# A layer norm's root moved to VectorE, a feature map in one tile, and an earlier modulation sum, in an attention and GLU kernel

## The chip, the cores and the metric

The kernel runs on one core of one Trainium2 chip. The metric is the device time of one execution in microseconds. A core has TensorE (PE: matmuls and transposes, with its weight loads as PEld), VectorE (DVE), ScalarE (ACT), GpSimd (POOL) and SyncE (SP), which here issues DMAs. Each engine works through its own instructions in order and waits at an instruction until the data and buffers it needs are ready.

## The reference

One block with conditioning: a modulation vector gives a shift, a scale and a gate for each of two halves. The first half is an attention over 4 segments of 512 tokens with 32 heads of width 16 and a running memory; the second a bilinear GLU. Sizes: x is 2048 × 512, the GLU's width 1376.

```python
mod = silu(c) @ w_mod                       # 6 vectors of 512: sa, ca, ga, sb, cb, gb
h = layernorm(x) * (1 + ca) + sa
# per segment s, q, k, v = h @ wq, h @ wk, h @ wv, 32 heads of 16
p = softmax(q @ k.T * scale + mask)         # inside the segment; masked where query < key
phi = lambda t: where(t > 0, t + 1, exp(t)) # feature map of the memory
a_mem = (phi(q) @ M) / (phi(q) @ z + 1e-6)  # memory of the earlier segments
o = g * a_mem + (1 - g) * (p @ v);  M += phi(k).T @ v;  z += sum(phi(k))
x = x + ga * (o @ wo)
h = layernorm(x) * (1 + cb) + sb
x = x + gb * (((h @ w_gate) * (h @ w_up)) @ w_down)
```

## The kernel before

The attention stage lasts from about 50 to 520 us and the GLU stage from there to the end; before 50 us weights are loaded and the first segment is projected. Attention is a loop over 32 half groups of 4 heads, each in 5 slots (0 to 4). A slot has a first score matmul `q` (queries against keys, which gives VectorE the row maxima `nm`), later a second one, `k`, with the maxima included, whose exponential on ScalarE is the tile `pt` (L329), which GpSimd masks with selects (L332); `tb` multiplies `pt` with the values.

Between these, a generator `fill_a` hands out work for the rest of the block: the projections `a_kq` of keys and queries of a segment (`kps`, `qps`, copied to `f`), the feature map phi, the memory `a_mem` (matmuls `mp`, `up`, `mz`), the layer norm of the next segment's rows (`ln_rows`, tiles `ast`, `amv`, `ay` and `x`; `cst`, `cmv`, `cy` for the norm in front of the GLU) and the modulation vectors. `weave(gen, other, places)` lets one step of `other` run at each listed yield of `gen`; a number listed twice takes two steps there. The order on TensorE is written out by these generators. The other engines are ordered by a scheduler, with some instructions pinned to where the program issues them (`pin`), or behind the last `pt` exponential (`behind`).

`ln_rows` takes the statistics of four row blocks (`BATCH_NORM_STATS2` and an aggregate, one step each), then Ln and Exp on ScalarE give 1/sqrt(var) as `y`, and one Newton step refines this root in five operations on 128 × 4 elements; only then is each block `x` normalized on VectorE. In the first norm of all, the five are on VectorE (`CV`), in the seven others on GpSimd (L187 to L191).

`mod_acc` makes one modulation vector from four blocks of `w_mod`: ScalarE scales block k by `s_c` (L626, in place, tile `wm`) and GpSimd adds it to block 0 (L628); the matmuls `mc` then turn the sum into columns. In segments 1 and 2 a second such vector is made inside the projections of group 1.

phi is built as min(exp(f), 1) + max(f, 0): ScalarE writes relu to `rl` (one buffer, L814) and the exponential to `ph` (L815), VectorE joins them later. The tile `f` has two buffers.

Of the kernel before, what the change touches and what calls it, by code (L numbers as in the profile page):

```python
# [9 lines left out]
F32 = mybir.dt.float32  # L10
F32R = mybir.dt.float32r
BF = mybir.dt.bfloat16
AF = mybir.ActivationFunctionType
ALU = mybir.AluOpType
# [4 lines left out]
P = 128  # L19
# [39 lines left out]
def tile_kernel(ctx, tc, x, wq, wk_, wv, wo, beta, w_gate, w_up, w_down, c, w_mod, out):  # L59
# [107 lines left out]
    def ln_rows(pool, xt, s, pfx):  # L167

        first = pfx == "a" and s == 0
        V, A = (CV, CA) if first else (vec, act)  # L170
        mv = pool.tile([P, 4, 2], F32, tag="mv", name=f"{pfx}mv{s}", bufs=2)
        for t in range(4):
            st = pool.tile([P, 6], F32, tag="st", name=f"{pfx}st{s}_{t}", bufs=2)
            i = V.bn_stats(st, xt[t])
            if not first:
                pin(i)
            V.bn_aggr(mv[:, t, :], st)
            if not first:
                yield 0.0
        sd = pool.tile([P, 4], F32, tag="sd", name=f"{pfx}sd{s}", bufs=2)  # L180
        A.activation(sd, mv[:, :, 1], AF.Ln, bias=epst[:, 0:1])
        y = pool.tile([P, 4], F32, tag="y", name=f"{pfx}y{s}", bufs=2)
        A.activation(y, sd, AF.Exp, scale=-0.5)
        a = pool.tile([P, 4], F32, tag="ya", name=f"{pfx}ya{s}", bufs=2)
        b = pool.tile([P, 4], F32, tag="yb", name=f"{pfx}yb{s}", bufs=2)
        eng = CV if first else nc.gpsimd
        eng.tensor_mul(a, y, y)  # L187
        eng.tensor_scalar(b, mv[:, :, 1], 1.0, EPS, op0=ALU.mult, op1=ALU.add)
        eng.tensor_mul(b, b, a)
        eng.tensor_scalar(b, b, -0.5, 1.5, op0=ALU.mult, op1=ALU.add)  # L190
        eng.tensor_mul(y, y, b)  # L191
        yield 0.0
        for t in range(4):
            i = V.tensor_scalar(xt[t], xt[t], mv[:, t, 0:1], y[:, t:t + 1],
                                op0=ALU.subtract, op1=ALU.mult)
            if not first:
                pin(i)
                yield 0.0
        if first:
            yield 0.0  # L200
# [382 lines left out]

    xts = {0: xload(0)}
    NWU = 20
    wu = pa.tile([P, 512], BF, tag="rl", name="wu", bufs=1)
    vec.memset(wu, 0.0)
    wups = psp.tile([P, 2, 512], F32, tag="lk", name="wups", bufs=1)

# [97 lines left out]
                i += 1  # L687

    wH, wL = {}, {}
    stage = [("ph", 3), ("ph", 3), ("ph", 3), ("mem", 2), ("pkr", 1), ("f", 2)] + [("x", 4)] * 6  # L690
    nst = [0]

    def staged(nm):
# [65 lines left out]
    def a_kq(s, g, nm):  # L759

        hH, hL = hcur[0]
        ph = phs.setdefault((s, g), {})
        if True:
            dst = kd if nm == "k" else qd
            ps = bank(f"{nm}ps{s}_{g}")
            n = 0
            for k in range(KT):
                for a, b in ((wH, hH), (wL, hH), (wH, hL)):
                    MM(ps, a[nm, g][:, k, :], b[k], start=n == 0, stop=n == 11)
                    n += 1  # L770
                    if n in (3, 6, 9):
                        yield 0.68
            give()
            f = pa.tile([P, L], F32, tag="f", name=f"{nm}f{s}_{g}", bufs=2)
            fast = s == 0 and g == 0
            A, V = (CA, CV) if fast else (act, nc.gpsimd)
            A.activation(f, ps, AF.Copy)
            q3 = pa.tile([P, 3, L], BF, tag="q3", name=f"{nm}3_{s}_{g}", bufs=2)
            r = pa.tile([P, L], F32, tag="qr", name=f"{nm}r_{s}_{g}", bufs=2)

            def part0():
                behind(A.activation(q3[:, 0, :], f, AF.Copy))
                V.tensor_sub(r, f, q3[:, 0, :])

            if fast:
                part0()
            else:
                keep(part0)

            def rest():  # L790
                (CV.tensor_copy if fast else act.copy)(q3[:, 1, :], r)
                V.tensor_sub(q3[:, 2, :], r, q3[:, 1, :])
                for r0, n, k in ((0, 3, 0), (3, 2, 0), (5, 1, 0)) if nm == "k" else ((0, 1, 3), (3, 1, 2), (5, 1, 1)):
                    if nm == "k":
                        nc.sync.dma_start(dst[s][g][r0:r0 + n].rearrange("r p t -> p r t"), q3[:, 0:n, :])
                    else:
                        i = 3 - k
                        nc.sync.dma_start(dst[s][g][r0:r0 + k].rearrange("r p t -> p r t"),
                                          q3[:, i:i + 1, :].to_broadcast([P, k, L]))

            if fast:
                rest()
            phi = (nm == "k" and s < NSEG - 1) or (nm == "q" and s > 0)
            if phi:
                if fast:
                    yield 0.0
                phlog.append((s, g, nm))
                while memq and (s == NSEG - 1 and g > 0 or len(phlog) > 3 and phlog[-4] not in phdone):
                    yield mem_step() or 0.0
                e = pa.tile([P, L], F32, tag="ph", name=f"ph{nm}{s}_{g}", bufs=3)  # L810
                rl = pa.tile([P, L], F32, tag="rl", name=f"rl{nm}{s}_{g}", bufs=1)

                def phi0():
                    behind(act.activation(rl, f, AF.Relu))  # L814
                    behind(act.activation(e, f, AF.Exp))  # L815

                if fast:
                    phi0()
                else:
                    keep(phi0)  # L820
                ph[nm] = e
            yield 0.68
            if not fast:
                give()
                rest()
            if phi:
                later.append([lambda: pin(vec.scalar_tensor_tensor(e, e, 1.0, rl, op0=ALU.min, op1=ALU.add)), 0, nm])
                if fast:
                    flush("kq")
        nkq[s, g] = nkq.get((s, g), 0) + 1  # L830
        if nkq[s, g] == 2:
            done.add((s, g))
# [127 lines left out]
    def fill_a():  # L960
# [5 lines left out]
        for s in range(NSEG):  # L966
# [4 lines left out]
            for g in range(2 if s == 0 else 0, NG):  # L971
                ws = []
                if s == 0 and g < 3:
                    ws = [load_g(nm, w, g + 1) for nm, w in (("k", wk_), ("q", wq))]
                for w in ws:
                    next(w)
                K, Q = a_kq(s, g, "k"), a_kq(s, g, "q")
                if g >= 2 and s + 1 < NSEG:
                    if g == 2:
                        xts[s + 1] = xload(s + 1)  # L980
                        lns = a_ln(s + 1)
                        K = weave(K, lns, (2, 3) if s > 0 else (3,))
                        Q = weave(Q, lns, (0, 1, 2) if s > 0 else (0, 1, 2, 3))
                    else:
                        K = weave(K, lns, (1, 1, 2, 2))
                        Q = weave(Q, lns, (0, 1, 2, 3))
                if g == 1 and 0 < s < 3:
                    acc = mod_acc(r)
                    K, Q = weave(K, acc, (0, 2)), weave(Q, acc, (0, 2))
                if s == NSEG - 1 and g == 1:  # L990
                    xr0 = xr_load(0, wpool, (0, 1), "wor")
                    ready = chain(wo_weights(), wo_op(0, None, B["orl"], us[0]))
                if s == NSEG - 1 and 0 < g < NG - 1:
                    K, Q = weave(K, ready, (0, 2)), weave(Q, ready, (0, 2) if g == 1 else (0, 2, 3))
                if s == NSEG - 1 and g == NG - 1:
                    yield from weave(Q, ready, (0, 1, 2, 3))
                    memq.append(a_mem(s, g))
                    yield from K
                    yield from ready
                    yield from wo_mm(0, us[0], xr0, (0, 1))  # L1000
                    break
                yield from K
                for w in ws:
                    next(w)
                yield from Q
                if s > 0 and g == 0:
                    while vfree[0] < s:
                        yield None
                    if s < 3:
                        yield from weave(a_v(s), mod_acc(r), (1, 3, 5, 7))  # L1010
                        yield from a_mod(2 * s, r[0])
                        r = load_mod(2 * s + 1)
                    else:
                        yield from a_v(s)
                        B["orl"] = wo_load(0, wpool)
                if g == 1 and 0 < s < 3:
                    yield from a_mod(2 * s + 1, r[0])
                memq.append(a_mem(s, g))
# [501 lines left out]
```

## Time and profile before

| What | Value |
| --- | --- |
| Median of 3 runs | 876.64 us |
| Lowest and highest | 872.87, 876.84 us |
| Profiled execution, its own time | 873.19 us |
| Its span in the trace | 871.1 us |
| Busy: PE, DVE, ACT, POOL | 828.9, 658.9, 474.5, 423.3 us |
| Mean granted clock of TensorE | 0.995 |

The span runs from the first to the last instruction in the trace; 2.1 us of the profiled execution lie outside it. Everything in the trace belongs to this one execution. A row of the timeline has the start in us, the duration, the engine, the line, the operation, what it writes and reads, and in brackets how long the engine had stood before it and what released it. In a window's row the granted clock is the share of TensorE's full clock that the throttle allowed.

### The profile page before, as it was taken

The numbers are of one execution on the slowest core, as the hardware profiler recorded it, in microseconds if no ns is written. First come the engines' busy times: TensorE is split into PE (matmuls) and PEld (weight loads), VectorE is DVE, ScalarE is ACT, GpSimd is POOL, SyncE is SP. The second block draws the span as 40 slices with busy tenths as digits, with TensorE's granted clock in tenths as the row PEclk, the third lists the DMA queues.
The fourth block names the chain that finished last, engine by engine and source line by source line (L and its number), as shares of the span: only waits on it lengthen the run. The fifth ranks groups of instructions, "written<-read, shape, count | busy, mean of one in ns | idle before, by whom it ended". The sixth has DMA issues, their size and how long they took to land.

```text
span 871.1 us, 14342 instructions
## 1 busy us (share of the span) xinstructions
PE 828.9 (95%) x4823; PEld 581.2 (67%) x4824; DVE 658.9 (76%) x1728; ACT 474.5 (54%) x740; POOL 423.3 (49%) x564
## 2 busy tenths in 40 slices
PE   8989998989999899999988899999999999999998
PEld 5756565656565566655654577888778888887886
DVE  8688776988779877789888769888685966767532
ACT  3758757687676876678544664433354423333321
POOL 4536536565455764487323835998101755650000
PEclk9999999999999999999999999999999999999999
DMA  7773755567647565776794552654305232112032
GB/s 242 227 233 120 226 149 168 187 209 232 194 147 250 188 205 168 250 235 215 235 310 134 170 173 97 181 159 135 109 30 163 77 115 55 50 55 94 0 119 97
DMA packets 111355, 139.45 MB, mean 160 GB/s; under 512 B 18800, under 2 KB 70000, under 8 KB 111280
## 3 DMA queue, kind: packets, MB, share of 16 engines
q1 hardware_dynamic: 106016, 130.91, 48.7%
q10 hardware_dynamic: 5264, 7.62, 2.4%
q8 instruction: 38, 0.62, 0.3%
q14 instruction: 37, 0.30, 0.1%
HBM read 87.48 MB, written 50.76 MB: 159 GB/s over the span
## 4 chain that ended last, share of the span: by engine, by line
PE 66%; DVE 13%; ACT 7%; DMA 5%; POOL 3%; issue 3%; SPq 0%; ACTq 0%; POOLq 0%; DVEq 0%
PE g L90 23%; PE acc L90 14%; PE tb L90 5%; PE k L90 5%; PE q L90 5%; DVE q L40 4%; PE vps L90 4%; PE kps L90 2%; ACT pt L329 2%; PE wops L90 2%; PE qps L90 2%; DVE x L40 2%; DMA x1d<-xr 1%; DMA x<-in_x_dram 1%; PE mz L90 1%
## 5 line engine op out<-in xcount | busy, mean ns | idle before, releaser
L40 DVE CUSTOM_DVE_ANT_0 q<-q,cmask 128x384 f32<-128x384 f32 (+3 forms) x512 | 246.6, 508 | 57.7 <-PE q L90 47.8
L329 ACT ACTIVATE pt<-k 128x1024 f32<-128x1024 f32 x160 | 163.9, 1024 | 74.2 <-PE k L90 57.3
L332 POOL TENSOR_SCALAR_AFFINE_SELECT pt<-pt 128x256 f32<-128x256 f32 (+1 forms) x224 | 105.2, 484 | 154.9 <-ACT pt L329 149.8
L90 PE MATMUL q<-kst,qst 96*128 96x384 bf16 (+3 forms) x512 | 101.6, 300 | 12.1 <-DVE nm L40 11.5
L90 PE MATMUL k<-qst,kst 98*128 98x384 bf16 (+3 forms) x512 | 97.5, 303 | 9.4 <-ACT pt L329 9.1
L448 POOL TENSOR_TENSOR w<-w 128x256 f32<-128x256 f32 (+1 forms) x84 | 73.9, 893 | 56.0 <-DVE t L1205 37.9
L443 POOL TENSOR_TENSOR AL<-w,AH 128x512 fp32r<-128x512 f32 (+1 forms) x42 | 56.4, 1345 | 48.4 <-ACT AH L439 48.3
L90 PE MATMUL tb<-pt,v 128*32 128x512 f32 (+3 forms) x1024 | 77.4, 443 | 1.4 <-POOL pt L332 1.4
L90 PEld LDWEIGHTS <-kst 98*128 98x128 bf16 x512 | 38.5, 99 | 54.3 <-issue 48.0
L40 DVE DVE_READ_ACCUMULATOR2_ANT nm<- 128x1 f32 x512 | 72.3, 141 | 0.0
L90 PEld LDWEIGHTS <-qst 96*128 96x128 bf16 x512 | 43.4, 98 | 39.9 <-issue 15.9
L439 ACT ACTIVATE AH<-w 128x512 fp32r<-128x512 f32 (+3 forms) x88 | 47.2, 565 | 40.0 <-POOL w L448 26.7
L1462 DVE TENSOR_TENSOR mL<-mid,mH 128x512 fp32r<-128x512 f32 (+1 forms) x44 | 32.8, 750 | 41.5 <-ACT mH L1461 41.5
L90 PE MATMUL acc<-DH,mL 128*128 128x512 f32 x144 | 56.6, 393 | 0.9 <-DVE mL L1462 0.9
L90 PE MATMUL acc<-DH,mH 128*128 128x512 f32 x144 | 57.2, 397 | 0.0
L90 PEld LDWEIGHTS tb<-pt,v 128*32 128x32 f32 x1024 | 29.2, 111 | 41.1 <-issue 36.1
L90 PE MATMUL acc<-DL,mH 128*128 128x512 f32 x144 | 56.6, 393 | 0.0
L1461 ACT ACTIVATE mH<-mid 128x512 fp32r<-128x512 f32 (+1 forms) x44 | 27.1, 627 | 52.7 <-PE acc L90 51.5
L1254 ACT ACTIVATE p<-g 128x512 f32<-128x512 f32 (+1 forms) x22 | 13.1, 597 | 75.9 <-PE g L90 75.8
L443 DVE TENSOR_TENSOR AL<-w,AH 128x512 fp32r<-128x512 f32 (+3 forms) x44 | 35.2, 803 | 9.2 <-ACT AH L439 9.0
L358 ACT ACTIVATE tsb<-tb 128x512 f32<-128x512 f32 x32 | 19.1, 598 | 34.0 <-PE tb L90 34.0
L90 PE MATMUL g<-chH,AH 128*128 128x512 f32 (+1 forms) x88 | 34.8, 396 | 0.7 <-ACT p L1254 0.7
(286 smaller groups left out, 2064.3 us busy)
## 6 DMA issues: line engine op xcount, KB each, us to landing
kst<-kd SPq DMA_DIRECT2D x32, 384.0 KB
qst<-qd SPq DMA_DIRECT2D x32, 384.0 KB
td<-tsb ACTq DMA_DIRECT2D x28, 256.0 KB
wm<-in_w_mod_dram SPq DMA_DIRECT2D x24, 256.0 KB
kd<-k SPq DMA_DIRECT2D x16, 384.0 KB
qd<-q SPq DMA_DIRECT2D x16, 384.0 KB
w<-in_w_gate_dram SPq DMA_DIRECT2D x20, 256.0 KB
w<-in_w_up_dram SPq DMA_DIRECT2D x40, 128.0 KB
```

What stands on the lines that cost most here:

```text
L40: i = getattr(self.eng, name)(*a, **k)
L90: return pe(nc.tensor.matmul(*a, **k))
L329: lpt[0] = act.activation(pt, kp, AF.Exp, scale=0.25)
L332: sels[u, i] = nc.gpsimd.affine_select(w, w, pattern=[[0, w.shape[1]], [1, P]], compare_op=ALU.is_ge, fill=0.0, base=0, channel_multiplier=-1)
L358: act.activation(tsbs[u], tbs.pop(u), AF.Copy)
L439: i = act.activation(hi[sl], w[sl], AF.Copy)
L443: i = eng.tensor_sub(lo[sl], w[sl], hi[sl].bitcast(F32))
L448: i = ce.tensor_tensor(w[:, o, :, 0:n], w[:, x, :, 0:n], w[:, y, :, 0:n], op=op)
L1254: lcp[0] = act.activation(r["p1"], ps, AF.Copy)
L1461: pin(act.activation(mH[0:n], md[0:n], AF.Copy))
L1462: vec.tensor_sub(mL[0:n], md[0:n], mH[0:n].bitcast(F32))
```

## The change

Four edits. The feature map becomes max(f, 0) + exp(−relu(−f)), which is the same function: ScalarE writes relu(−f) to `ph` and the exponential in place, the tile `rl` is gone, and VectorE reads `f` itself, which therefore is held longer and gets a third buffer. The root of the seven later norms is refined on VectorE in four operations (two of the five are joined in one), pinned ahead of the first normalization; the step's yield moves ahead of them. The norm of segment 1's rows, woven into segment 0's third group, takes its statistics steps at other yields: none in K, five in Q. And the second modulation vector of segments 1 and 2 takes three of its four steps in K (yields 1, 2, 3) and one in Q, where it had two in each. The startup tile `wu` shares another tag.

```diff
         b = pool.tile([P, 4], F32, tag="yb", name=f"{pfx}yb{s}", bufs=2)
-        eng = CV if first else nc.gpsimd
-        eng.tensor_mul(a, y, y)
-        eng.tensor_scalar(b, mv[:, :, 1], 1.0, EPS, op0=ALU.mult, op1=ALU.add)
-        eng.tensor_mul(b, b, a)
-        eng.tensor_scalar(b, b, -0.5, 1.5, op0=ALU.mult, op1=ALU.add)
-        eng.tensor_mul(y, y, b)
-        yield 0.0
+        if not first:
+            yield 0.0
+        for i in (V.tensor_mul(a, y, y), V.scalar_tensor_tensor(b, mv[:, :, 1], EPS, a, op0=ALU.add, op1=ALU.mult),
+                  V.tensor_scalar(b, b, -0.5, 1.5, op0=ALU.mult, op1=ALU.add), V.tensor_mul(y, y, b)):
+            if not first:
+                pin(i)
+        if first:
+            yield 0.0
...
-    wu = pa.tile([P, 512], BF, tag="rl", name="wu", bufs=1)
+    wu = pa.tile([P, 512], BF, tag="qr", name="wu", bufs=2)
...
-            f = pa.tile([P, L], F32, tag="f", name=f"{nm}f{s}_{g}", bufs=2)
+            f = pa.tile([P, L], F32, tag="f", name=f"{nm}f{s}_{g}", bufs=3)
...
                 e = pa.tile([P, L], F32, tag="ph", name=f"ph{nm}{s}_{g}", bufs=3)
-                rl = pa.tile([P, L], F32, tag="rl", name=f"rl{nm}{s}_{g}", bufs=1)
 
                 def phi0():
-                    behind(act.activation(rl, f, AF.Relu))
-                    behind(act.activation(e, f, AF.Exp))
+                    behind(act.activation(e, f, AF.Relu, scale=-1.0))
+                    behind(act.activation(e, e, AF.Exp, scale=-1.0))
...
-                later.append([lambda: pin(vec.scalar_tensor_tensor(e, e, 1.0, rl, op0=ALU.min, op1=ALU.add)), 0, nm])
+                later.append([lambda: pin(vec.scalar_tensor_tensor(e, f, 0.0, e, op0=ALU.max, op1=ALU.add)), 0, nm])
...
-                        K = weave(K, lns, (2, 3) if s > 0 else (3,))
-                        Q = weave(Q, lns, (0, 1, 2) if s > 0 else (0, 1, 2, 3))
+                        K = weave(K, lns, (2, 3) if s > 0 else ())
+                        Q = weave(Q, lns, (0, 1, 2) if s > 0 else (0, 1, 2, 2, 3))
...
-                    K, Q = weave(K, acc, (0, 2)), weave(Q, acc, (0, 2))
+                    K, Q = weave(K, acc, (1, 2, 3)), weave(Q, acc, (0,))
```

TensorE's order is the same in both kernels. VectorE's, around the statistics of segment 1's rows (`ast_0` to `ast_3` of `x_0` to `x_3`) near 58 us, before; `ISA q_3_0` is the maximum of slot 3 of the first head pair, and each writes a column of `nm`:

```order
115 L40 BN_STATS ast_1_802<-x_1_692 128x6
116 L40 BN_AGGR amv_775<-ast_1_802 128x2
117 L40 BN_STATS ast_2_808<-x_2_694 128x6
118 L40 BN_AGGR amv_775<-ast_2_808 128x2
119 L40 ISA q_3_0_814,nm_738<-q_3_0_814,cmask 128x384
```

And now, from slot 3's last maximum on:

```order
122 L40 ISA q_3_1_812,nm_735<-q_3_1_812,cmask 128x128
123 L40 ISA nm_735 128x1
124 L40 SCALAR_TENSOR_TENSOR phk_2_770<-kf_2_766,phk_2_770 128x512
125 L40 BN_STATS ast_2_825<-x_2_691 128x6
126 L40 BN_AGGR amv_794<-ast_2_825 128x2
127 L40 BN_STATS ast_3_828<-x_3_693 128x6
128 L40 BN_AGGR amv_794<-ast_3_828 128x2
129 L40 ISA q_4_0_861,nm_735<-q_4_0_861,cmask 128x256
```

The statistics of `x_2` stood ahead of slot 3's maxima and now stand behind them and behind the feature map's combination. Those of `x_0` likewise moved from ahead of slot 2's maxima to behind them.

VectorE's order where the same norm is applied, near 68 us, now:

```order
152 L40 ISA nm_888 128x1
153 L40 TENSOR_TENSOR aya_842<-ay_840 128x4
154 L40 SCALAR_TENSOR_TENSOR ayb_843<-amv_794,aya_842 128x4
155 L40 TENSOR_SCALAR ayb_843<-ayb_843 128x4
156 L40 TENSOR_TENSOR ay_840<-ay_840,ayb_843 128x4
157 L40 TENSOR_SCALAR x_0_687<-x_0_687,amv_794,ay_840 128x512
158 L40 TENSOR_SCALAR x_1_689<-x_1_689,amv_794,ay_840 128x512
```

Rows 153 to 156 are new there; what is around them is as before, and the five rows on GpSimd are gone. It is the same in the six other norms.

GpSimd's order around the second modulation vector of segment 1, near 140 us, before and then now (`wm_0` is the sum, `pt_2` to `pt_4` the masked exponentials of slots 2 to 4, `kr` and `k` the parts of the projected keys):

```order
95 L332 AFFINE_SELECT pt_2_1774<-pt_2_1774 128x2x128 x2
96 L783 TENSOR_TENSOR kr_1_1766<-kf_1_1763,k_1_1_1765 128x512
97 L332 AFFINE_SELECT pt_3_1819<-pt_3_1819 128x2x128 x2
98 L628 TENSOR_TENSOR wm_0_1675<-wm_0_1675,wm_2_1679 128x512
99 L792 TENSOR_TENSOR k_1_1_1765<-kr_1_1766,k_1_1_1765 128x512
100 L628 TENSOR_TENSOR wm_0_1675<-wm_0_1675,wm_3_1681 128x512
101 L332 AFFINE_SELECT pt_4_1843<-pt_4_1843 128x4x128
```

```order
90 L629 TENSOR_TENSOR wm_0_1667<-wm_0_1667,wm_2_1671 128x512
91 L333 AFFINE_SELECT pt_2_1765<-pt_2_1765 128x2x128 x2
92 L784 TENSOR_TENSOR kr_1_1758<-kf_1_1755,k_1_1_1757 128x512
93 L629 TENSOR_TENSOR wm_0_1667<-wm_0_1667,wm_3_1673 128x512
94 L333 AFFINE_SELECT pt_3_1812<-pt_3_1812 128x2x128 x2
95 L793 TENSOR_TENSOR k_1_1_1757<-kr_1_1758,k_1_1_1757 128x512
96 L333 AFFINE_SELECT pt_4_1836<-pt_4_1836 128x4x128
```

Each of the two sums moved from behind a slot's selects to ahead of them. On ScalarE the scalings moved in the same way: that of `wm_2` stands ahead of `pt_2`'s exponential and that of `wm_3` ahead of `pt_3`'s, where both stood behind `pt_3`'s.

More of the change, by code (lines that the diff above doesn't have):

```diff
@@ L689, in tile_kernel @@
     wH, wL = {}, {}
-    stage = [("ph", 3), ("ph", 3), ("ph", 3), ("mem", 2), ("pkr", 1), ("f", 2)] + [("x", 4)] * 6
+    stage = [("ph", 3), ("ph", 3), ("ph", 3), ("mem", 2), ("pkr", 1), ("f", 3)] + [("x", 4)] * 6
     nst = [0]
```

## The prediction

> **What bounds the kernel now.** I read the page first, then the busy time by stage, then who TensorE waits for, then the timeline around the longest of those waits. The page's first part and the windows by stage (time, then busy time and count of PE, PEld, DVE, ACT, POOL, then the granted clock) give the frame.
>
> ```profile
> span 871.1 us, 14342 instructions
> PE 828.9 (95%) x4823; PEld 581.2 (67%) x4824; DVE 658.9 (76%) x1728; ACT 474.5 (54%) x740; POOL 423.3 (49%) x564
> 50.00:520.00 470.00, 439.69 (x3106) 274.20 (x3106) 376.87 (x1284) 323.35 (x471) 257.93 (x379) 0.99 0.64 200
> 520.00:871.00 351.00, 344.53 (x1505) 276.55 (x1504) 243.84 (x351) 126.17 (x230) 142.57 (x141) 1.00 0.31 96
> ```
>
> TensorE is the bound everywhere, and only the attention stage, with 30.3 us of idle PE in 470, has something to give; after 520 us it is busy for 344.5 of 351, so nothing that moves on another engine there can matter by a microsecond. The list of waits says where the 30 us lie.
>
> ```profile
> PE q L90 <- DVE nm L40: 11.5, 23, 1.6
> PE mc L90 <- POOL wm L628: 2.4, 1, 2.4
> PE ctp L93 <- DVE x L40: 1.3, 1, 1.3
> ```
>
> The first is the score matmul that waits for VectorE's row maxima (`nm`); the change touches it from both sides. The second is one wait, which the change aims at. Two places stand out in the timeline (start, duration, instruction, idle before it and its releaser). Place B, the layer norm of segment 1's rows woven into segment 0; the last two rows are windows (PE's busy time, the granted clock, the DMA share, GB/s):
>
> ```profile
> 58.22 0.69 DVE L40 BATCH_NORM_STATS2 ast<-x 128x6 f32<-128x512 f32 x1 [1.68 <-DMA x<-in_x_dram]
> 61.41 0.69 DVE L40 BATCH_NORM_STATS2 ast<-x 128x6 f32<-128x512 f32 x1
> 60.09 0.38 PE L90 MATMUL q<-kst,qst 96*128 96x256 bf16 x2 [1.59 <-DVE nm L40]
> 61.00 0.59 PE L90 MATMUL q<-kst,qst 96*128 96x256 bf16 x2 [0.53 <-DVE nm L40]
> 61.38 2.02 PE L90 MATMUL mz<-v,pkr 128*128 128x136 f32 x8
> 149.98 1.20 PE L90 MATMUL mz<-v,pkr 128*128 128x136 f32 x8
> 60.00:62.00 2.00, 1.38 (x7) 0.69 0.69 242
> 62.00:64.00 2.00, 2.00 (x9) 0.50 0.09 29
> ```
>
> VectorE stands 1.68 us for the third row block to arrive, with the maxima of slot 3 queued behind it; TensorE stands 1.59 + 0.53. Then the granted clock is 0.50, and eight `mz` matmuls take 2.02 us where the same eight take 1.20 at 149.98. Place E, the modulation columns of segment 1:
>
> ```profile
> 144.12 1.05 PE L90 MATMUL mc<-ones,wm 128*128 128x1 f32 x8 [2.43 <-POOL wm L628]
> 146.00 4.05 PE L90 MATMUL tb<-pt,v 128*32 128x512 f32 x32
> 469.42 2.36 PE L90 MATMUL tb<-pt,v 128*32 128x512 f32 x32
> 135.42 1.02 ACT L329 ACTIVATE pt<-k 128x1024 f32<-128x1024 f32 x1
> 138.18 1.02 ACT L329 ACTIVATE pt<-k 128x1024 f32<-128x1024 f32 x1
> 139.09 0.73 ACT L626 ACTIVATE wm<-wm,s_c 128x512 f32<-128x512 f32 x1
> 140.21 0.73 ACT L626 ACTIVATE wm<-wm,s_c 128x512 f32<-128x512 f32 x1
> 140.01 1.28 POOL L628 TENSOR_TENSOR wm<-wm,wm 128x512 f32<-128x512 f32 x1
> 141.24 1.16 POOL L792 TENSOR_TENSOR k<-kr,k 128x512 bf16<-128x512 f32 x1
> 142.35 1.72 POOL L628 TENSOR_TENSOR wm<-wm,wm 128x512 f32<-128x512 f32 x1
> 146.00:148.00 2.00, 2.00 (x13) 0.53 1.01 358
> ```
>
> The last sum on GpSimd ends at 142.35 + 1.72 = 144.07 and TensorE starts at 144.12. Again half clock follows, and 32 `tb` matmuls take 4.05 us where 32 take 2.36 elsewhere: 1.7 us.
>
> **The change part by part.** The base is the profiled execution, 873.19 us, close to the fastest of the three runs shown; the median, 876.64, is 3.45 above it, which is about two more losses like the 1.7 us at place E. That reading is a guess, since only one run has a trace. A measurement tells about 0.5% from nothing, 4.4 us.
>
> Weave of the norm (place B). Now the maxima of slots 2 and 3 go ahead of the statistics of blocks 0 and 2, one place each. VectorE stood from 56.54 (58.22 − 1.68); from 58.22 to 61.41 it then ran, in 3.19 us, block 2's statistics, slot 3's maxima and the feature-map combination. In the new order the same work starts at 56.54 with the maxima and comes to block 2 last, at about 58.9, when it is there (58.22). Block 3's turn is at 59.73 instead of 61.41: 1.7 us sooner, the removed wait. Is block 3 there by then?
>
> ```profile
> 52.41 0.35 SPq L580 DMA_DIRECT2D x<-in_x_dram  x1
> 54.93 0.62 SPq L580 DMA_DIRECT2D x<-in_x_dram  x1
> ```
>
> The last of the four loads is issued at 54.93, and the row at 61.41 did not wait for it, so waiting for it costs between 0 and 1.7. Block 2's load took 5.8 us from its issue at 52.41 to 58.22; the same for block 3 would be 60.7, a wait of 1.0. It has less traffic behind it, the DMA share falling from 0.69 to 0.09 after 62, and I take 0. TensorE loses both its waits (2.1) and the half clock (0.8 on `mz`, some more after it), but VectorE then sets the end, so I take 1.7, from 0.7 (late block) to 3.3 (VectorE catches up).
>
> Modulation sums (place E). The scalings of blocks 2 and 3 go ahead of the exponentials of slots 2 and 3, and GpSimd's sums ahead of those slots' selects. Step by step: ACT scales block 2 at 135.4, where slot 2's exponential stood, which moves back by about 0.6. Block 3 comes where slot 3's exponential stood, at 138.18, with one scaling more ahead of it and the feature map's exponential (0.6) less, so at about 138.3 instead of 140.21. On GpSimd the sum with block 2 (1.28, as at 140.01) is done by 137.5; the sum with block 3 has slot 2's selects and a subtraction like that at 141.24 (1.16) ahead of it, and I estimate its end at 140.6, or 141.0 if it takes the 1.72 of 142.35. TensorE comes to `mc` at 144.12 − 2.43 = 141.69. The whole 2.43 goes, and with it, by the rows, the half clock: 1.7. What is queued behind the moved work is slot 3's exponential, later by at most 0.7 and needed by a score matmul three slots' work on; I take nothing, with 0.6 as its worst. Segment 2's sums had no wait and change nothing. E: −4.1, between −1.8 (0.6 lost, clock not regained) and −4.1.
>
> [...]
>
> Root on VectorE. Five small GpSimd operations of seven norms become four on VectorE, immediately ahead of the normalization that needs them. The first norm, which has them on VectorE already, gives their price.
>
> ```profile
> 9.99 0.17 DVE L40 TENSOR_TENSOR aya<-ay 128x4 f32<-128x4 f32 x1 [0.36 <-ACT ay L40]
> 10.89 1.00 DVE L40 TENSOR_SCALAR x<-x,amv,ay 128x512 f32<-128x512 f32 x2
> 74.23 0.38 PE L90 MATMUL q<-kst,qst 96*128 96x256 bf16 x2 [0.53 <-DVE nm L40]
> 174.89 3.94 DVE L40 TENSOR_SCALAR x<-x,amv,ay 128x512 f32<-128x512 f32 x4
> 179.82 0.38 PE L90 MATMUL q<-kst,qst 96*128 96x512 bf16 x1 [1.38 <-DVE nm L40]
> 180.72 0.38 PE L90 MATMUL q<-kst,qst 96*128 96x512 bf16 x1 [0.53 <-DVE nm L40]
> 180.00:182.00 2.00, 1.47 (x9) 1.00 0.95 333
> 289.16 0.38 PE L90 MATMUL q<-kst,qst 96*128 96x256 bf16 x2 [0.53 <-DVE nm L40]
> 477.16 0.33 PE L93 MATMUL ctp<-ident,x 128*128 128x128 f32 x1 [1.29 <-DVE x L40]
> 503.43 1.00 DVE L40 TENSOR_SCALAR x<-x,cmv,cy 128x512 f32<-128x512 f32 x2 [5.63 <-POOL cy L191]
> ```
>
> Five took 0.90 from 9.99 to 10.89, 0.18 each: four are 0.72, and the first norm saves 0.2 on a chain that nothing covers. At 74, 180, 289 and 477 TensorE already waits for VectorE, right behind such a normalization, so the 0.72 goes through: 4 × 0.72 = 2.9, at least 0 if VectorE's slack returns, at most 2.9. At 503 VectorE had waited 5.63 for GpSimd's root; that goes, but the list of waits has TensorE waiting for `x` only once, at 477, so I take nothing. The two norms after 520 us are covered by a full TensorE. At 180 the wait of 1.38 becomes 2.10, with 0.53 behind it; place B's 1.59 with 0.53 was followed by half clock, this one (clock 1.00) was not. I take one new loss of 1.7 there; at 477 (1.29 to 2.01) none.
>
> Feature map and buffers. Relu now writes `ph` and the exponential follows in place: as many ScalarE instructions of the same size, and the combination on VectorE has the same shape.
>
> ```profile
> 137.38 0.62 ACT L815 ACTIVATE phk<-kf 128x512 f32<-128x512 f32 x1
> 142.07 0.87 DVE L40 SCALAR_TENSOR_TENSOR phk<-phk,rlk 128x512 f32<-128x512 f32 x1
> ```
>
> The exponential ends 4.1 us ahead of its reader, which covers the exponential of scores (1.02) that is now often ahead of it; without that cover it would cost up to 1.0 in one place. `f` is held until VectorE's combination, a third buffer pays for that. Zero, ±0.5 for the reordering.
>
> Sum: 873.19 − 0.2 (first norm) − 1.7 (B) − 4.1 (E) + 2.9 (root) + 1.7 (half clock at 180) = 871.8.
>
> **The rivals.** (1) No new half clock at 180: 871.8 − 1.7 = 870.1, and 868.5 if VectorE catches up after B, so that B is worth 3.3 and not 1.7. For it: the waits of 1.29 and 1.38 kept a clock of 1.00. Against: what followed place B's 1.59 and 0.53. (2) The root gives the gain back: half clock at 477 too, and block 3 late by 1.0, which is the case in which the new weave does not do what it is written for: 871.8 + 1.7 + 1.0 = 874.5, and 875.1 with slot 3's 0.6 at E. For it: VectorE is the laggard in all four places. Against: the forecast's order leaves block 3 4.8 us from its issue, and only the load behind the wait at 58.22 is known to have taken longer. (3) Slower: the root makes VectorE the bound, and its longer waits halve the clock wherever they stand. Without the root's 2.9 and the 1.7 the sum is 867.2. If a wait of 1.25 (0.53 + 0.72) already halves the clock, all four places lose 0.72 + 1.7, in sum 9.7: 876.9. If each draws a second stretch of half clock behind it, 16.5: 883.7. It decides at about 1.2 us of waiting; the 1.29 and 1.38 that kept their clock speak against it. (4) The waits do not set the clock: then neither the 1.7 at E is won nor that at 180 lost, 871.8 as well, with half clock still near 146. The 0.50 and 0.53 behind the two longest losses speak against it. [...]
>
> **How the numbers follow.** The forecast has 0.38 and (4) 0.05, both at 871.8, with a range of their own from 870 to 874; (1) has 0.25, (2) 0.20, (3) 0.12. Faster by over 0.5% of the median is under 872.3: all of (1) and six tenths of the forecast and (4), 0.25 + 0.26 = 0.51. Slower is over 881.0: the upper case of (3), 0.08. The rest, 0.41, is within 0.5%. The range from 867 to 877.5 adds 1.5 below (1)'s 868.5, for a root that VectorE's slack hides in two places, takes in (2) and the lower case of (3), and leaves out the upper.
>
> **What would show it.** In the profile after: no VectorE wait for `x` near 58, and q's waits at 60 and 61 under 0.8; `mc` without a wait and `tb` behind it at 2.4; four root operations of 0.17 ahead of `x`; the waits at 180 and 477 near 2.1 and 2.0; half clock, if anywhere, near 180. The prediction is wrong if `mc` still waits, if half clock stays near 146, if VectorE waits for block 3, or if a new wait for `pt` or `ph` appears.

## The result and the profile after

The changed kernel is slower: 885.24 us (median of 11 runs, 879.44 to 888.58) against 876.84 (11 runs, 872.87 to 883.48), a ratio of 1.0083 with a 95% interval from 1.006 to 1.0106. The ratios on record differ a little from the quotients of the medians (here 1.0096); where a run below is said to be some us slower or faster, that is its ratio times the median of before. The forecast was 871.8, with a range from 867 to 877.5. The profiled execution took 888.38 us, near the top of its runs, as that of before (873.19) was near the bottom of its own; the two traces therefore differ by 15.2 us, nearly twice the medians' difference of 8.4.

The page's busy times, the waits of TensorE, and one matmul near the start of the GLU stage, before and then now:

```profile
span 886.7 us, 14336 instructions
PE 838.8 (95%) x4824; PEld 583.3 (66%) x4824; DVE 671.4 (76%) x1755; ACT 475.0 (54%) x740; POOL 415.7 (47%) x529
PE q L90 <- DVE nm L40: 17.3, 26, 3.1
PE k L90 <- ACT pt L330: 7.2, 11, 2.4
523.73 0.50 PE L90 MATMUL g<-chH,AH 128*128 128x512 f32 x1 [0.75 <-ACT p L1254]
537.49 0.51 PE L90 MATMUL g<-chH,AH 128*128 128x512 f32 x1 [0.75 <-ACT p L1254]
```

That matmul comes 13.8 us later, and the spans differ by 15.6: attention has lost 13.8 us, and 1.8 more are lost in the GLU stage. TensorE waits 5.8 us more for the maxima and is busy for 10 us more with the same matmuls, most of it because the granted clock over the span fell from 0.995 to 0.987 (0.008 of 886.7 is 7.1). The wait of `mc` is gone. VectorE is busy for 12.5 us longer, where 27 more operations of 0.18 make 4.9. That remainder is the clue. Here is the root at 172, with GpSimd's rows beside it, what TensorE waited for, and the clock behind it (PE's busy time, the clock, DMA share, GB/s):

```profile
172.53 0.16 DVE L40 TENSOR_TENSOR aya<-ay 128x4 f32<-128x4 f32 x1
172.73 1.09 DVE L40 SCALAR_TENSOR_TENSOR ayb<-amv,aya 128x4 f32<-128x4 f32 x1
173.85 0.17 DVE L40 TENSOR_SCALAR ayb<-ayb 128x4 f32<-128x4 f32 x1
174.06 0.40 DVE L40 TENSOR_TENSOR ay<-ay,ayb 128x4 f32<-128x4 f32 x1
174.50 3.72 DVE L40 TENSOR_SCALAR x<-x,amv,ay 128x512 f32<-128x512 f32 x4
172.64 1.16 POOL L793 TENSOR_TENSOR q<-qr,q 128x512 bf16<-128x512 f32 x1
174.04 0.41 POOL L333 TENSOR_SCALAR_AFFINE_SELECT pt<-pt 128x256 f32<-128x256 f32 x1 [0.24 <-ACT pt L330]
179.20 0.38 PE L90 MATMUL q<-kst,qst 96*128 96x512 bf16 x1 [3.12 <-DVE nm L40]
180.00:182.00 2.00, 1.90 (x6) 0.54 0.42 151
182.00:184.00 2.00, 2.00 (x10) 0.61 0.15 53
```

The second operation has as few elements as the others and takes 1.09 us: it ends at 173.82, and GpSimd's subtraction at 172.64 + 1.16 = 173.80. The fourth ends with the select, at 174.46 and 174.45. The profile shows this standing as a longer instruction, not as idle time. The root takes 1.97 us from 172.53 to 174.50, the wait at 180 is 3.12, not 2.10, and half clock follows. The same happens at 290:

```profile
289.86 1.09 DVE L40 SCALAR_TENSOR_TENSOR ayb<-amv,aya 128x4 f32<-128x4 f32 x1
289.77 1.16 POOL L784 TENSOR_TENSOR qr<-qf,q 128x512 f32<-128x512 f32 x1
```

Places B and E, and a third that the prediction did not have, at 385:

```profile
59.89 0.68 DVE L40 BATCH_NORM_STATS2 ast<-x 128x6 f32<-128x512 f32 x1
60.70 0.66 DVE L40 BATCH_NORM_STATS2 ast<-x 128x6 f32<-128x512 f32 x1
62.54 0.38 PE L90 MATMUL q<-kst,qst 96*128 96x512 bf16 x1 [1.57 <-DVE nm L40]
64.00:66.00 2.00, 2.00 (x9) 0.52 0.06 20
143.52 0.95 PE L90 MATMUL mc<-ones,wm 128*128 128x1 f32 x8
145.29 2.36 PE L90 MATMUL tb<-pt,v 128*32 128x512 f32 x32
385.68 2.15 DVE L40 SCALAR_TENSOR_TENSOR phq<-qf,phq 128x512 f32<-128x512 f32 x1
392.07 0.58 PE L90 MATMUL q<-kst,qst 96*128 96x256 bf16 x2 [3.03 <-DVE nm L40]
392.00:394.00 2.00, 1.61 (x8) 0.50 0.95 284
```

At B the statistics of blocks 2 and 3 did not wait for their loads, but the wait came back at 62.5, with half clock behind it. At E the wait and the half clock are gone, as forecast. At 385 the feature map's combination took 2.15 us, where it takes 0.69 with GpSimd idle, and two operations behind it 1.65 and 1.76.

Two more losses stand where the prediction had none: half clock behind the wait for `x` (1.29 at 477 before), and a wait in the GLU stage, where the root at 585, ahead of two normalizations that took 2.96 us beside GpSimd and 1.42 before, makes VectorE late with `u`:

```profile
489.79 0.33 PE L93 MATMUL ctp<-ident,x 128*128 128x128 f32 x1 [1.48 <-DVE x L40]
492.00:494.00 2.00, 2.00 (x10) 0.50 0.84 202
590.33 0.50 PE L90 MATMUL g<-t_0H,AH 128*128 128x512 f32 x1 [0.94 <-DVE u L1263]
```

By the starts of the same matmuls in the two traces, the changed kernel loses 0.7 us at B, gains 3.9 at E, and loses 3.3 at 180, 1.5 at 199 (a wait for `pt`), 1.6 at 268 (half clock), 1.3 at 290, 4.9 at 385, 2.3 near 440 (a longer wait for `pt`, and half clock) and 1.8 in the GLU stage; the rest is in steps of about 1 or less.

### The profile page after: what moved, and what is told of

It reads as the page before. It is cut to its first block, busy times and chain, and to the rows that moved or that the text cites. A ratio compares the mean times of both kernels' runs of the same rounds, so it can differ in the third digit from the quotient of the medians.

```text
span 886.7 us, 14336 instructions
## 1 busy us (share of the span) xinstructions
PE 838.8 (95%) x4824; PEld 583.3 (66%) x4824; DVE 671.4 (76%) x1755; ACT 475.0 (54%) x740; POOL 415.7 (47%) x529
## 4 chain that ended last, share of the span: by engine, by line
PE 60%; DVE 18%; DMA 7%; ACT 5%; POOL 5%; issue 4%; SPq 0%; ACTq 0%; DVEq 0%; POOLq 0%
PE g L90 18%; PE acc L90 14%; DVE q L40 6%; PE tb L90 5%; PE q L90 5%; PE k L90 5%; PE vps L90 3%; PE kps L90 3%; PE qps L90 2%; POOL w L449 2%; ACT pt L330 2%; DVE x L40 2%; PE wops L90 1%; DMA qst<-qd 1%; DVE nm L40 1%
## 5 line engine op out<-in xcount | busy, mean ns | idle before, releaser
L330 ACT ACTIVATE pt<-k 128x1024 f32<-128x1024 f32 x160 | 163.9, 1024 | 75.6 <-PE k L90 63.8
L90 PE MATMUL q<-kst,qst 96*128 96x384 bf16 (+3 forms) x512 | 104.6, 304 | 19.8 <-DVE nm L40 17.3
L449 POOL TENSOR_TENSOR w<-w 128x256 f32<-128x256 f32 (+1 forms) x84 | 72.1, 871 | 57.4 <-DVE t L1205 37.9
L444 POOL TENSOR_TENSOR AL<-w,AH 128x512 fp32r<-128x512 f32 (+1 forms) x42 | 59.1, 1410 | 48.9 <-ACT AH L440 47.5
L444 DVE TENSOR_TENSOR AL<-w,AH 128x512 fp32r<-128x512 f32 (+3 forms) x44 | 33.2, 757 | 12.1 <-ACT AH L440 12.0
L90 PE MATMUL g<-t_0H,AH 128*128 128x512 f32 (+1 forms) x88 | 35.2, 400 | 1.7 <-DVE u L1263 1.2
```

The lines of the kernel that those rows point to most:

```text
L90: return pe(nc.tensor.matmul(*a, **k))
L330: lpt[0] = act.activation(pt, kp, AF.Exp, scale=0.25)
L444: i = eng.tensor_sub(lo[sl], w[sl], hi[sl].bitcast(F32))
L449: i = ce.tensor_tensor(w[:, o, :, 0:n], w[:, x, :, 0:n], w[:, y, :, 0:n], op=op)
```

## The experiments

The theory from this trace (A): the root is the loss, because VectorE's operations stand while GpSimd works. Its rivals: the feature map (B), or no single part but their sum (C). The first four kernels do one part of the change each.

**The root alone** (the diff's hunk in `ln_rows`):

```diff
-        eng = CV if first else nc.gpsimd
-        eng.tensor_mul(a, y, y)
...
+        for i in (V.tensor_mul(a, y, y), V.scalar_tensor_tensor(b, mv[:, :, 1], EPS, a, op0=ALU.add, op1=ALU.mult),
```

> The kernel before with the root of the seven norms on VectorE and nothing else. Theory A (VectorE's root operations stand while GpSimd works, 1.09 us where 0.16 was counted, and the longer waits halve the clock): 5 to 9 us slower than before, at least three roots with an operation of about 1 us, new half clock near 180. Theory B (the feature map is what costs): 2 to 3 us slower, as the prediction had the root. Theory C (no part alone costs much, only their sum shifts the phases): within 3 us.

890.65 us (median of 4 runs) against 875.5, ratio 1.0172 (1.0153 to 1.0191): 15.1 us slower, more than A gave it and more than the whole change. TensorE's wait for the maxima is 18.7 us in sum. Three of the seven roots have operations of 1.1 to 1.2 us, at 179, 297 and 516:

```profile
179.66 1.07 DVE L40 SCALAR_TENSOR_TENSOR ayb<-amv,aya 128x4 f32<-128x4 f32 x1
297.05 1.10 DVE L40 SCALAR_TENSOR_TENSOR ayb<-amv,aya 128x4 f32<-128x4 f32 x1
301.89 0.38 PE L90 MATMUL q<-kst,qst 96*128 96x256 bf16 x2 [2.25 <-DVE nm L40]
206.65 0.60 PE L90 MATMUL k<-qst,kst 98*128 98x384 bf16 x4 [1.59 <-ACT pt L330]
```

The last row is a loss that comes 20 us later: with the root on VectorE the scheduler gives ScalarE its work in another order, and an exponential of scores comes late. Half clock followed it in this trace.

**The feature map alone:**

```diff
-                    behind(act.activation(rl, f, AF.Relu))
-                    behind(act.activation(e, f, AF.Exp))
+                    behind(act.activation(e, f, AF.Relu, scale=-1.0))
+                    behind(act.activation(e, e, AF.Exp, scale=-1.0))
```

> The kernel before with the feature map in one tile and the third buffer of f and nothing else. Theory A: within 2 us of before. Theory B (the exponential comes later on ScalarE and GpSimd's order moves, so that VectorE's combination falls beside GpSimd operations, 2.15 us at 385 where 0.77 was): 4 to 8 us slower, with a wait of about 3 us of the score matmul near 380. Theory C: within 3 us.

877.27, ratio 1.0015 (0.9997 to 1.0033): no difference that can be told. B falls. The combination at 381 took 1.47 there and TensorE waited 0.72 behind it, so the 3.03 of the changed kernel comes from where the phases stood, not from this edit alone. The traces do hold a sign of a cost near 440: half clock behind a wait for `pt` of 1.91 to 2.37 us stands there in the three kernels with this edit (this one, the whole change but the root, and the whole change) and in none of the nine others.

**The weave alone:**

```diff
-                        K = weave(K, lns, (2, 3) if s > 0 else (3,))
-                        Q = weave(Q, lns, (0, 1, 2) if s > 0 else (0, 1, 2, 3))
+                        K = weave(K, lns, (2, 3) if s > 0 else ())
+                        Q = weave(Q, lns, (0, 1, 2) if s > 0 else (0, 1, 2, 2, 3))
```

> The kernel before with the norm of segment 1 woven in at the new places and nothing else. The prediction's term: 1.7 us faster. Rival: the wait comes back as the wait of the next group's score matmul (1.57 at 62.5 in the changed kernel) with half clock behind it, so no gain, within 1 us of before.

874.93, ratio 0.9996 (0.9978 to 1.0015). The rival is right: the waits at 60 and 61 are gone, and the same two stand at the score matmuls of the next group, nearly 4 us later.

```profile
63.84 0.38 PE L90 MATMUL q<-kst,qst 96*128 96x512 bf16 x1 [1.59 <-DVE nm L40]
64.75 0.38 PE L90 MATMUL q<-kst,qst 96*128 96x512 bf16 x1 [0.53 <-DVE nm L40]
66.00:68.00 2.00, 2.00 (x11) 0.50 0.00 0
```

**The modulation sums alone:**

```diff
-                    K, Q = weave(K, acc, (0, 2)), weave(Q, acc, (0, 2))
+                    K, Q = weave(K, acc, (1, 2, 3)), weave(Q, acc, (0,))
```

> The kernel before with the modulation sums sooner and nothing else. The prediction's term: the 2.43 us wait of the column matmuls goes and the half clock behind it, 4.1 us faster. Rival: the gain is lost within 40 us, since the score matmul near 179 waits for VectorE anyway and its wait grows by as much (3.12 in the changed kernel against 1.38): 0 to 1.5 us faster, half clock moved from 146 to 180.

872.21, ratio 0.9957 (0.9942 to 0.9973): 3.8 us faster, the prediction's term of 4.1. The wait is gone and the clock behind it is full:

```profile
143.47 0.95 PE L90 MATMUL mc<-ones,wm 128*128 128x1 f32 x8
145.24 2.36 PE L90 MATMUL tb<-pt,v 128*32 128x512 f32 x32
146.00:148.00 2.00, 2.00 (x32) 1.00 0.94 333
```

The next four put the root apart from what leaves GpSimd, and try the change without it. **Without the Newton step** (no root operations on either engine in the seven norms):

```diff
+        for i in () if not first else (V.tensor_mul(a, y, y), V.scalar_tensor_tensor(b, mv[:, :, 1], EPS, a, op0=ALU.add, op1=ALU.mult),
```

> The kernel before in which the seven later norms leave the Newton step of the root out altogether; the yields stand as in the kernel with the root on VectorE, and GpSimd is as free as there. Theory A (VectorE's four operations are the cost): within 2 us of before. Theory D (not the operations, but what leaves GpSimd and shifts the other orders, costs): 5 us or more slower than before, near the root alone.

878.62 against 876.29, ratio 1.0026 (0.9997 to 1.0055), 2.3 us, at the edge of A's 2. So relieving GpSimd and moving the yield do not cost the 15 us, and on GpSimd the root had cost nothing that could be won back. D falls.

**The root on VectorE in the attention norms only** (`on_v = first or pfx == "a"`, with the five GpSimd operations kept where it is false):

> The root on VectorE in the three later attention norms alone, on GpSimd in the four norms ahead of the GLU; all else as before. By the prediction's term (0.72 in each place) 2.2 us slower. By theory A, from the changed kernel's trace (1.9 at 180 and 290, the wait of 3.1 and one half clock of 1.7 after each of the three): 8 to 11 us slower. The rest of the root alone, 4 to 7, would then be the GLU norms'.

885.45 (4 runs), ratio 1.0114 (1.0089 to 1.014): 10 us slower, within A's 8 to 11, where the prediction's term gave 2.2. VectorE's busy time is 655.5 here, 3.4 less than before, although two of its three roots have an operation of 1.1 us: a total that does not grow is no proof that nothing stands.

**The weave and the modulation sums together**, and **the whole change but the root:**

> The weave and the modulation sums without the root and the feature map. If the parts add up (0.9996 and 0.9957): 4 us faster than before, 871.4. If the half clock at 180 follows the earlier arrival: 2 us faster.

> The changed kernel with the root left on GpSimd in five operations. If the root is the whole loss: 2.5 to 4 us faster than before (parts: -0.4, -3.7, +1.3). If the parts disturb one another (theory C): slower than before.

871.21, ratio 0.9951 (0.9925 to 0.9977), and 872.6, ratio 0.9968 (0.9946 to 0.999). Both beat both kernels; the first has the lowest ratio found, 4.3 us below before, nearly all of it the modulation sums, whose 3.8 its interval takes in. C falls for the three parts without the root: they do not disturb one another. With the root they do: the wait of 3.03 near 385, with its half clock, stands in the changed kernel alone, and no other has more than 1.23 there.

What remained was what about the root costs so much: any four operations more on VectorE at those places (E), or that they stand beside GpSimd (A). VectorE's operations in the twelve traces can be sorted by whether a GpSimd operation ran as they began. RECIPROCAL, the statistics, the maxima and operations with one operand in PSUM (`u`, `xr`, `MZ`) have the same median beside GpSimd as alone, within 0.03; the others, with all operands in SBUF, do not (`phq` 0.69 alone and 1.14 beside, `mL` 0.69 and 1.22, `xn` 0.54 and 0.96). **Four reciprocals in the place of the four operations**, at the same size:

```diff
+        for i in (...) if first else (V.reciprocal(a, y), V.reciprocal(b, a), V.reciprocal(a, b), V.reciprocal(y, a)):
```

> The root alone, with its four operations replaced by four reciprocals of the same 128x4 size at the same places (the fourth gives the first's input back, so the Newton step is left out). In the four traces so far a RECIPROCAL took the same time beside a GpSimd operation as alone (0.35 and 0.35 for rd), while the root's operations took up to 1.2 beside one. Theory A, in its sharper form (VectorE's operations with all operands in SBUF wait for the running GpSimd operation): the four take about 0.8 us in each norm, no one above 0.3, and the kernel is 3 to 6 us slower than before. Theory E (any four operations more on VectorE at these places cost this, by the half clock that the longer waits bring): as the root alone, 12 to 16 us slower.

880.61 against 876.39, ratio 1.0037 (1.0015 to 1.0059): 3.2 us slower. The reciprocals are not held up by the same GpSimd operation, and TensorE's wait at 180 is what it was before:

```profile
175.28 0.17 DVE L40 RECIPROCAL aya<-ay 128x4 f32<-128x4 f32 x1
175.48 0.18 DVE L40 RECIPROCAL ayb<-aya 128x4 f32<-128x4 f32 x1
175.69 0.18 DVE L40 RECIPROCAL aya<-ayb 128x4 f32<-128x4 f32 x1
175.91 0.18 DVE L40 RECIPROCAL ay<-aya 128x4 f32<-128x4 f32 x1
175.37 1.16 POOL L793 TENSOR_TENSOR q<-qr,q 128x512 bf16<-128x512 f32 x1
180.20 0.38 PE L90 MATMUL q<-kst,qst 96*128 96x512 bf16 x1 [1.38 <-DVE nm L40]
198.97 0.60 PE L90 MATMUL k<-qst,kst 98*128 98x384 bf16 x4 [1.38 <-ACT pt L330]
74.63 0.38 PE L90 MATMUL q<-kst,qst 96*128 96x256 bf16 x2 [0.53 <-DVE nm L40]
480.94 0.33 PE L93 MATMUL ctp<-ident,x 128*128 128x128 f32 x1 [1.36 <-DVE x L40]
```

Same engine, count, size and places: 3.2 us. Operations that stand beside GpSimd: 15.1. The difference, some 12 us, is the standing and what follows from it (longer waits, half clock). ScalarE's other order is no part of it: the reciprocals have it too, with the wait of 1.38 for `pt` at 199. By the starts of the same matmuls, the root alone loses on the reciprocals 3.3 us at its wait of 3.12 and the half clock behind it, 1.6 in the half clock at 208, 2.9 at the wait of 2.25 near 302 and its half clock, and 1.6 in the GLU stage; the rest is mostly half clock near 17 and 147, which lasts longer in one trace than in the other. E falls.

**The root on VectorE in the four norms ahead of the GLU only** (`on_v = first or pfx == "c"`):

> The root on VectorE in the four norms ahead of the GLU alone. If the parts add up, the root alone less the attention norms: 15 - 10 = 5 us slower than before. By the prediction's term 0.7 slower. In the trace: the root of the second norm, near 510, takes over 2 us beside GpSimd, and the wait for x near 477 is near 2.

878.52, ratio 1.0022 (1.0001 to 1.0043): 1.9 us, less than the 5 expected. The root near 504 took 2.8 us, as expected, but the wait for `x` is 1.36 and not 2, and what the same matmuls lose is 1.6 in the GLU stage. The two halves give 10.0 and 1.9, together 3 less than the root alone; and with the other three parts the root costs 10 (from 0.9968 to 1.0083), not 15. Why it costs more by itself is open; each kernel's half clock falls in other places.

## Why the prediction was wrong

The step that failed is the root's price, 0.72 in each of four places and one new half clock, 4.6 us in sum; measured were 15.1 alone and 10 with the other parts. I took 0.18 per operation from the first norm, at 9.99 to 10.89, where nothing on GpSimd was longer than 0.21 us, and carried it to places where GpSimd runs subtractions of 1.16. Measured there: 1.97 instead of 0.72 at 172, 1.7 at 290 and 3.3 at 511. The trace of before held the warning, in an operation that I used only for its length. These are two rows of before, with one of the same kind alone:

```profile
161.64 1.43 DVE L40 SCALAR_TENSOR_TENSOR phk<-phk,rlk 128x512 f32<-128x512 f32 x1
161.37 1.16 POOL L792 TENSOR_TENSOR k<-kr,k 128x512 bf16<-128x512 f32 x1 [0.37 <-ACT k L791]
60.81 0.69 DVE L40 SCALAR_TENSOR_TENSOR phk<-phk,rlk 128x512 f32<-128x512 f32 x1
```

1.43 is the 0.89 until GpSimd ends at 162.53, and then most of its own 0.69. The root in the changed kernel shows the same: its second operation takes 1.09 at 172.73, where GpSimd's subtraction ends at 173.80, and 0.16 at 585.90, where GpSimd is idle. The reciprocals were not held up: 0.17 to 0.18 each, the last three inside a subtraction of 1.16. Why the one waits and the other does not was not shown.

Point by point. The 2.9 for the root's work as such meets the 3.2 (1.3 to 5.2) of the reciprocals by luck: where nothing is held up, the waits at 74, 180 and 477 do not grow by 0.72 (0.53, 1.38 and 1.36, from 0.53, 1.38 and 1.29), and a wait for `pt` comes at 199, where I had nothing. The new half clock at 180 came, behind a wait of 3.12 and not 2.10. At 477 I had no half clock, and it came, as in rival (2), behind 1.48. That the norms after 520 us are covered was wrong: TensorE waits 0.93 to 0.94 for `u`, between 580 and 595, in the three kernels that have the root of these norms refined on VectorE, and in none of the others.

The modulation term held, 3.8 of 4.1, the half clock with it: it follows the wait for `mc` in all eight kernels that have that wait, and is absent in the four that do not. The weave's 1.7 was wrong: I had seen that VectorE would set the end, but not that the wait then moves whole to the next score matmul, and in three of the four kernels with the new weave takes the half clock along; block 3 was in time. The first norm's 0.2 did not show: its root took 0.85, from 10.54 to 11.39, instead of 0.90, and began 0.55 later. The feature map cost nothing to be told in the medians. Rival (3) came nearest, the root that makes VectorE the bound, but for another reason than its 0.72.

On the clock, half clock followed 2.43 us without work in before (0.53 from 146 to 148), and 1.59 with 0.53 behind it in weave alone (0.50 from 66 to 68). But the length of a wait did not decide alone. At 180, a wait of 1.35 to 1.39 with 0.53 behind it kept a clock of 1.00 in before and in five other kernels, and half clock followed it in three; and 1.59 with 0.53 was not followed by it in the kernel with the weave and the modulation sums. This is one of the three, the kernel without the Newton step:

```profile
180.70 0.38 PE L90 MATMUL q<-kst,qst 96*128 96x512 bf16 x1 [1.38 <-DVE nm L40]
182.00:184.00 2.00, 2.00 (x9) 0.50 0.81 292
```

So the two waits that kept their clock in before, 1.29 and 1.38, were weak ground for the forecast's one new half clock. What decides besides the length was not tried.

## What to carry to other kernels

A duration carries over only to places with the same neighbours: here the same operation took 0.16 alone and 1.09 beside a GpSimd subtraction of 1.16. Before a small operation is moved to VectorE, look up what GpSimd runs at the new place, and price it at the longest of those. If VectorE's busy time grows by more than the added operations times their length, as here by 12.5 us where they make 4.9, look in the rows for operations that stand; if it does not grow, as with the root in the attention norms alone (3.4 less than before), look at the rows all the same. A wait that was removed from an engine's feeder without giving the feeder time moved to the next consumer (1.59 and 0.53, from 60 and 61 to 63.8 and 64.8); a sum that was merely late, as at E, gave its whole wait of 2.43 back.

## What the runs showed of the hardware

With few exceptions, VectorE operations with two inputs in SBUF, and fp32 scalings from SBUF to SBUF, that began beside a GpSimd operation ended only when it had ended. Of the root, 128 × 4, in the changed kernel: with two inputs 0.16 alone at 585.90, 1.09 at 172.73 and 1.20 at 513.70, each ending 0.01 to 0.02 behind GpSimd's; the scaling 0.17 alone at 586.10 and 0.56 at 513.10, ending 0.02 behind a select. Exceptions in that trace: from 694.15 to 696.97 five with two inputs took 0.41 to 0.68 inside one GpSimd operation, which itself lasted 4.44.

RECIPROCAL, the statistics and operations that read one operand from PSUM did not wait: `rd` took 0.35 at 227.19 in before, inside a sum of 1.27, `ast` 0.68 at 59.89 now, inside a subtraction of 1.56, and `u` 0.68 at 574.26 in before, inside one of 1.50. Near 180, waits of TensorE of 1.35 to 1.39 us with 0.53 behind them were followed by half clock in three kernels and not in six. And on GpSimd five small operations had been free: leaving the root out altogether made the kernel no faster (ratio 1.0026, from 0.9997 to 1.0055).
